# An attention and MLP kernel: softmax normalisation by 32x32 VectorE transposes, four heads of scores per round, and zero matmuls before the input arrives

## The chip, the cores and the metric

The kernel runs on one core of one Trainium2 chip. The metric is the device time of one execution in microseconds (us), as a median over runs. Five engines work side by side: TensorE (PE in the profile; PEld is its weight load), VectorE (DVE), ScalarE (ACT), GpSimd (POOL) and SyncE (SP), which here issues most of the DMAs. TensorE's clock is throttled: the trace has records of a granted clock that is either full or half (in the kernel before, matmuls of 512 columns stand 216 ns apart at full clock and 427 at half).

The kernel before takes 235.04 us (median of three runs, 234.85 to 235.3).

## The reference, cut to what matters

```python
x = A_x                                          # 1 x 2048 x 448, bf16
h  = x + _A_ref(_layernorm(x), A_wqkv, A_wo)     # 16 heads of 28; each query sees 8 keys, every second one back
h2 = h + _B_ref(_layernorm(h), w1, w2, w3, w4)   # token mixing, then an MLP of width 1792
# inside _A_ref
logits = jnp.where(mask, jnp.einsum("bhsd,bhswd->bhsw", q, kg) * scale, -1e9)
attn = _softmax(logits, axis=-1)
o = jnp.einsum("bhsw,bhswd->bhsd", attn, vg)
return o.transpose(...).reshape(B, S, D) @ wo
```

The kernel works on four tiles of 512 tokens, numbered 0 to 3. For each tile: layer norm (A1), transposition of the normalised tile into `hT`, V and QK projections, attention in four groups of four heads (att, av), output projection (WO), a second layer norm (B1), and so on to the MLP (W3, B3). Tile 0 is transposed by TensorE, the others by a DMA transpose. Even and odd tokens lie in different tiles, so that the dilated window becomes a band.

## The kernel before

The 3,650 or so instructions are not written in their order. The program lists operations with estimated durations, and a list scheduler, run when the kernel is built, fixes the order of every engine. Its estimates: a matmul always costs its time at full clock, and a DMA lands after bytes over a fixed bandwidth plus 2 us.

```python
def mm(out_ap, lhsT, rhs, start, stop, n, mode="full"):
    return S.add("pe", "matmul", n / 2.4 + 3 if mode == "full" else 26.0, ...)

    # in _Sched.schedule(self, dma_bw=180.0, slack=100.0): of the ready operations take the one that can start
    # first, ties by rank in _ORDER, a list of some 170 stage names
            if op.is_dma:
                free[e] = st + op.dur
                ts = max(st + op.dur, dma_free[e])
                dma_free[e] = ts + op.lat / dma_bw
                op.t1 = dma_free[e] + 2000.0
            else:
                op.t1 = st + op.dur
                free[e] = op.t1
            order[e].append(op)          # from here on the order is fixed
```

The statistics of a layer norm go from VectorE to GpSimd (a power and three small operations), and each of the four normalisations of a tile to VectorE or ScalarE, whichever the plan has free:

```python
def phase_A1(t):
    for i in range(4 * t, 4 * t + 4):
        ln_stats(0, xin[:, i, :], i)                 # VectorE
        if t == 0:
            inv_std(0, 0, i, 1)                      # GpSimd: four serial chains for tile 0
    if t > 0:
        inv_std(0, 0, 4 * t, 4)
    for il in range(4):
        normalize_t(0, 0, 4 * t + il, ls, il, xin[:, 4 * t + il, :])   # VectorE or ScalarE
    ...
    if t == 0: transposes(ls, hT[:, par, :, :])      # TensorE
    else:      transpose_dma(ls, hT[:, par, :, :])   # DMA
```

Attention, for each group c of four heads. The values have a 29th column that is constant, so row 28 of each 32-row block of the output is the softmax sum:

```python
for jp in range(2):                                  # two heads per round, two PSUM banks
    T = tile(2)
    for q0, nq, k0 in BLK:
        for j in (2 * jp, 2 * jp + 1):
            mm(T(... a=j % 2 ...), qk[32 * j:32 * j + 28, par, c, 1, k0:k0 + KB],
               qk[32 * j:32 * j + 28, par, c, 0, 8 + q0:8 + q0 + nq], True, True, nq, "rows")
    act(pj, T(...), ACT.Exp, 1024, scale=SCALE)
    dve("tensor_tensor", 1024, 2.0, out=pj, in0=pj, in1=m_, op=ALU.mult)        # mask
... # 20 matmuls of attention times V into O; after every second group:
if c % 2 == 1:
    copy(osb[:, par, c - 1:c + 1, :], O(lambda p: p[:, :, :]), 1024)
... # once per tile, after its four groups:
dma("zg%d" % par, zp[:, par, :], zrows, 32768)                      # gather the sums
dve("reciprocal", 400, out=rzp[:, par, :], in_=zp[:, par, :])
dve("tensor_scalar", 64, out=rzp[:, par, :], in0=rzp[:, par, :], scalar1=UP, ...)
dma("zs%d" % par, zd.rearrange("j (r n) -> (j r) n", n=64), rzp[:, par, :], 32768)   # to DRAM
for j in range(4):                                                  # and back, to 32 rows each
    dma("zb%d" % j, rzb[32 * j:32 * j + 32, :, :]..., bass.AP(rz_d, ..., [[0, 32], [1, 2048]]), 32 * 8192)
for c in range(4):
    dve("tensor_tensor", 512, out=oT[:, par, c, :], in0=osb[:, par, c, :], in1=rzb[:, c, :], op=ALU.mult)
```

## Time and profile before

| What | Value | Read from |
|---|---|---|
| time, median | 235.04 us | runs |
| span of the profiled run | 232.0 us | page |
| TensorE busy | 201.1 us, 87% | page, part 1 |
| VectorE, ScalarE, GpSimd busy | 121.6, 117.2, 66.4 us | page, part 1 |
| first real matmul | 13.83 us | timeline |
| 848 full-array matmuls, 189 or 216 ns apart | 171.5 us | trace |
| half clock between the first real matmul and the tail (no record yet counts as half) | 14.5 us | clock records of the trace |
| TensorE's waits from 14 us on | 14.9 us | timeline, sum of the brackets |

TensorE is the engine to look at: it is busy nearly throughout and its clock is sometimes halved. From the page of the kernel before, the span, the busy line and two rows of the table of 40 slices (5.8 us each; the digit is the busy share in tenths, and for PEclk the granted clock in tenths):

```profile
span 232.0 us, 3657 instructions
PE 201.1 (87%) x1505; PEld 102.6 (44%) x1505; DVE 121.6 (52%) x244; ACT 117.2 (50%) x131; POOL 66.4 (29%) x123
PE   0289999999999749499778999999999999999992
PEclk9999999999999967889999999999999999999998
```

The PE row shows an empty start, a thin stretch in slices 14 to 22 (75 to 128 us) and a dense second half. PEclk shows a 9 also where there is no record yet: the first one, of a full clock, stands at 18.13 us, and matmuls before it ran 427 ns apart, at half speed. The timeline of TensorE in the kernel before (start, duration, what, count; in brackets the idle time before it and what ended that):

```profile
6.77 0.46 PE L1197 MATMUL ps<-ident,lntm 128*112 128x128 bf16 x2 [6.77 <-ACT lntm L1197]
...
11.39 1.32 PE L1197 MATMUL ps<-ident,lntm 128*112 128x128 bf16 x10 [1.18 <-DVE lntm L1197]
13.83 6.38 PE L1197 MATMUL ps<-hT,arena 112*128 112x512 bf16 x19 [1.12 <-ACT hT L1197]
```

The transposes of tile 0 come first, then 19 matmuls in 6.38 us, the first of them at half speed. The softmax round trip is seen in the DMA queue's timeline of the kernel before:

```profile
81.85 0.55 SPq L1197 DMA_DIRECT2D zp<-arena  x1
85.27 0.34 SPq L1197 DMA_DIRECT2D rz_scratch<-rzp  x1
86.73 1.70 SPq L1197 DMA_DIRECT2D rzb<-rz_scratch  x4
88.47 4.68 SPq L1197 DMA_TRANSPOSE actT<-lntm  x1
```

This is the third of four tiles: the sums are gathered at 81.85 us, written at 85.27, fetched back from 86.73, and the transposition that follows in the queue comes behind them. Two groups of VectorE in the kernel before, which the change removes (count | busy us, mean ns | idle before):

```profile
L1197 DVE TENSOR_TENSOR oT<-arena,rzb 128x512 bf16<-128x512 f32 x16 | 11.0, 737 | 1.0 <-DMA rzb<-rz_scratch 1.0
L1197 DVE RECIPROCAL rzp<-zp 128x64 f32<-128x64 f32 x4 | 2.2, 547 | 0.3 <-DMA zp<-arena 0.3
```

### The profile page before, as it was taken

The page shows a single profiled execution, that of the slowest core. Times are in us where ns is not written, and L with a number is a line of the kernel's source. Part 1 is how long each engine was busy: PE and PEld are TensorE (multiplying, and loading weights), DVE is VectorE, ACT ScalarE, POOL GpSimd, SP SyncE. Part 2 cuts the span into 40 slices and gives each one's busy share as a digit, 9 for nine tenths or more (in the row PEclk, how much of TensorE's full clock was granted, in tenths as well). Part 3 has the DMA queues.
Part 4 walks back from the last instruction along what each step waited for, and adds up shares of the span by engine and source line. Part 5 has one row for each costly group of instructions (what it writes and reads, how often), then busy time and mean ns, then how long its engine had stood idle before and what let it go on. Part 6 is the DMA issues. An engine that isn't in the chain of part 4 may idle for free.

```text
span 232.0 us, 3657 instructions
## 1 busy us (share of the span) xinstructions
PE 201.1 (87%) x1505; PEld 102.6 (44%) x1505; DVE 121.6 (52%) x244; ACT 117.2 (50%) x131; POOL 66.4 (29%) x123
## 2 busy tenths in 40 slices
PE   0289999999999749499778999999999999999992
PEld 0135564445456424254333455554444455444550
DVE  6494684458859888956889604992100122001221
ACT  2616885578877795495651663214755500353000
POOL 8856374001100610433183500489700000000000
PEclk9999999999999967889999999999999999999998
DMA  5925615976604309447504040041400501001111
GB/s 159 298 66 147 154 28 113 277 241 123 158 6 113 79 11 193 87 83 184 100 8 86 0 90 0 3 90 59 90 3 0 110 20 41 21 0 41 41 45 47
DMA packets 31671, 19.82 MB, mean 85 GB/s; under 512 B 24800, under 2 KB 30256, under 8 KB 31136
## 3 DMA queue, kind: packets, MB, share of 16 engines
q1 hardware_dynamic: 30608, 15.10, 29.0%
q0 software_dynamic: 1040, 4.42, 6.8%
q8 instruction: 14, 0.23, 0.4%
q14 instruction: 9, 0.07, 0.1%
HBM read 11.65 MB, written 1.97 MB: 59 GB/s over the span
## 4 chain that ended last, share of the span: by engine, by line
PE 64%; DVE 14%; ACT 7%; DMA 6%; POOL 5%; issue 2%
PE ps L1197 64%; DVE st L1197 5%; DMA actT<-lntm 4%; ACT pt L1197 3%; POOL rstd L1197 3%; DMA hT<-lntm 3%; DVE xin L1197 3%; POOL nmr L1197 2%; DVE mv L1197 1%; ACT arena L1197 1%; DVE xb L1197 1%; DVE pt L1197 1%; POOL vtmp L1197 1%; ACT qk L1197 1%; DVE lntm L1197 1%
## 5 line engine op out<-in xcount | busy, mean ns | idle before, releaser
L1197 PE MATMUL ps<-actT,w_s 112*128 112x512 bf16 (+1 forms) x288 | 67.5, 386 | 2.8 <-DMA actT<-lntm 2.8
L1197 ACT ACTIVATE arena<-ps 128x1024 bf16<-128x1024 f32 (+1 forms) x34 | 34.8, 1023 | 43.5 <-PE ps L1197 43.3
L1197 DVE TENSOR_TENSOR xb<-ps,xb 128x448 bf16<-128x448 f32 (+1 forms) x24 | 18.3, 771 | 65.5 <-PE ps L1197 65.5
L1197 PEld LDWEIGHTS ps<-actT,w_s 112*128 112x128 bf16 (+1 forms) x288 | 30.4, 107 | 35.5 <-DMA actT<-lntm 4.3
L1197 PE MATMUL ps<-w_s,arena 128*128 128x448 bf16 x224 | 45.0, 353 | 0.0
L1197 PE MATMUL ps<-hT,arena 112*128 112x512 bf16 x128 | 32.0, 400 | 1.5 <-ACT hT L1197 1.1
L1197 ACT ACTIVATE pt<-ps 110x1024 bf16<-110x1024 f32 x32 | 30.5, 1023 | 4.5 <-PE ps L1197 4.4
L1197 PEld LDWEIGHTS ps<-w_s,arena 128*128 128x128 bf16 x224 | 21.9, 98 | 21.2
L1197 DVE TENSOR_TENSOR pt<-pt,msk 110x1024 bf16<-110x1024 bf16 x32 | 21.0, 683 | 12.6 <-ACT pt L1197 12.6
L1197 POOL TENSOR_SCALAR vtmp<-mv 128x4 f32<-128x4 f32 (+1 forms) x19 | 5.2, 276 | 67.9 <-DVE mv L1197 67.0
L1197 DVE BATCH_NORM_STATS2 st<-xin 128x6 f32<-128x448 bf16 x32 | 19.3, 604 | 0.7 <-issue 0.5
L1197 PEld LDWEIGHTS ps<-hT,arena 112*128 112x128 bf16 x128 | 12.1, 102 | 16.9 <-issue 2.8
L1197 POOL TENSOR_TENSOR rstd<-vtmp,mhalf 128x4 f32<-128x4 f32 (+1 forms) x19 | 19.0, 999 | 1.6
L1197 PE MATMUL ps<-wo_s,oT 128*128 128x448 bf16 x64 | 15.2, 393 | 2.9 <-DVE oT L1197 1.7
L1197 POOL TENSOR_TENSOR xb<-xb,xin 128x448 bf16<-128x448 bf16 x16 | 16.7, 1073 | 2.4 <-DVE lntm L1197 1.5
L1197 ACT ACTIVATE lntm<-xin,nmr,rstd 128x448 bf16<-128x448 bf16 x16 | 11.5, 755 | 10.3 <-POOL nmr L1197 10.3
L1197 PE MATMUL ps<-qk 28*110 28x103 bf16 (+1 forms) x320 | 12.1, 220 | 4.8 <-ACT arena L1197 2.6
L1197 ACT ACTIVATE qk<-ps 128x1024 bf16<-128x1024 f32 x10 | 10.2, 1024 | 10.7 <-PE ps L1197 10.7
L1197 PE MATMUL ps<-arena,hT 112*110 112x448 bf16 x64 | 14.9, 358 | 0.4 <-DMA hT<-lntm 0.4
L1197 PE MATMUL ps<-w_s,gT 112*128 112x448 bf16 x64 | 12.8, 353 | 1.4 <-ACT gT L1197 1.4
L1197 PEld LDWEIGHTS ps<-qk 28*110 28x110 bf16 x320 | 9.2, 127 | 10.0 <-ACT arena L1197 3.3
L1197 ACT ACTIVATE gT<-ps 112x1024 bf16<-112x1024 f32 x8 | 8.2, 1024 | 9.0 <-PE ps L1197 9.0
(58 smaller groups left out, 162.7 us busy)
## 6 DMA issues: line engine op xcount, KB each, us to landing
rzb<-rz_scratch SPq DMA_DIRECT2D x16, 256.0 KB, 4.5
w_s<-in_B_w_dram POOLq DMA_DIRECT2D x2, 1568.0 KB, 11.5
out_dram<-xb SPq DMA_DIRECT2D x16, 112.0 KB, 1.7
xin<-in_A_x_dram SPq DMA_DIRECT2D x3, 448.0 KB, 7.9
arena<-in_A_wqkv_dram SPq DMA_DIRECT2D x3, 392.0 KB, 5.3
w_s<-in_B_w_dram POOLq DMA_DIRECT2D x2, 392.0 KB, 4.6
xin<-in_A_x_dram SPq DMA_DIRECT2D x4, 112.0 KB, 2.2
wo_s<-in_A_wo_dram POOLq DMA_DIRECT2D x4, 98.0 KB, 2.5
```

Of the source, the lines that this page charges most:

```text
L1197: inst = getattr(eng, op.meth)(**op.kw)
```

## The change

The intent: keep the softmax sums out of DRAM. A 32x32 transpose on VectorE turns each block of 29 rows by 32 queries so that the sum stands beside its query, where a reciprocal and a broadcast product normalise it; a second transpose turns the block back. Besides: the scores of four heads go in one round on four PSUM banks, tile 0's statistics are taken in pairs, and 14 zero matmuls are to have the clock up when the input arrives. The list of priorities is a new one, so nearly every engine's order changes. The diff, cut to its core:

```diff
-W3_0.04 W3_0.10 W3_0.02 W3_2 ...
+W3_2.04 W3_2.00 W3_2.12 W3_2.08 ...                                  [all 13 lines of _ORDER]
+    WARM = 14
+    zz = sb("zz", [128, 512], BF16)
+    dve("memset", 256, ap=zz[:], constant=0.0)
-            if t == 0:
-                inv_std(0, 0, i, 1)
+            if t == 0 and i % 2 == 1:
+                inv_std(0, 0, i - 1, 2)
...                                                                   [scores]
+            Ts = [tile(2), tile(2)]
+            for q0, nq, k0 in BLK:
+                for j in range(4):
+                    mm(Ts[j // 2](lambda p, a=j % 2, q=q0, n=nq: p[0:KB, a, q:q + n]), ...
             for jp in range(2):
-                T = tile(2)
-                for q0, nq, k0 in BLK:
-                    for j in (2 * jp, 2 * jp + 1):
-                        mm(T(lambda p, a=j % 2, q=q0, n=nq: p[0:KB, a, q:q + n]), ...
-                act(pj, T(lambda p: p[0:KB, :, :]), ACT.Exp, 1024, scale=SCALE)
+                act(pj, Ts[jp](lambda p: p[0:KB, :, :]), ACT.Exp, 1024, scale=SCALE)
...                                                                   [normalisation, two groups at a time]
-                copy(osb[:, par, c - 1:c + 1, :], O(lambda p: p[:, :, :]), 1024)
-        [the gather, the reciprocal, the write, four reads back and four products of the kernel before]
+                dve("transpose", 1024, psum=True, out=of[:, os_, :, :], in_=O(lambda p: p[:, :, :]))
+                o4 = of[:, os_, :, :].rearrange("p u (b d) -> p (u b) d", d=32)
+                dve("reciprocal", 160, out=rz[:, os_, :], in_=o4[:, :, 28])
+                dve("scalar_tensor_tensor", 1024, out=ob[:, os_, :, :]...,
+                    in0=rz[:, os_, :].unsqueeze(2).broadcast_to([128, 32, 32]), scalar=UP, in1=o4, op0=ALU.mult, op1=ALU.mult)
+                dve("transpose", 1024, out=oT[:, par, c - 1:c + 1, :], in_=ob[:, os_, :, :])
...                                                                   [zero matmuls]
+    S.tag = "warm"
+    T = tile()
+    for _ in range(WARM):
+        mm(T(lambda p: p[:, 0, :]), zz[:, 0:128], zz[:], True, True, 800)
     phase_A1(0)
```

A few estimated durations were also corrected (a normalisation on ScalarE from 560 to 755 ns, for example).

More of the change, by code (lines that the diff above doesn't have):

```diff
@@ L20, in __init__ @@
     def __init__(self, idx, eng, meth, kw, dur):
-        self.idx = idx; self.eng = eng; self.meth = meth; self.kw = kw; self.dur = dur
+        self.idx = idx; self.eng = eng; self.meth = meth; self.kw = kw; self.dur = float(int(dur))
         self.deps = set(); self.users = 0; self.sem = None; self.val = 0
@@ L103, in add @@
         if chan is not None:
-            op.is_dma = True; op.chan = chan; op.lat = float(lat)
+            op.is_dma = True; op.chan = chan; op.lat = float(int(lat))
             self.chan_count[chan] = self.chan_count.get(chan, 0) + 1
@@ L256, in schedule @@
                 op.meth, op.kw, op.dur = op.opts[e]
+                op.dur = float(int(op.dur))
             if e == "act" and op.table is not None:
@@ L338 @@
 _ORDER = """
-W3_0.04 W3_0.10 W3_0.02 W3_2 W3_2.10 W3_2.00 W3_2.04 W3_2.08 W3_3.12 W3_3.02 W3_3.08 W3_3.06 B2_0.0 B2_0.2 W3_3
-W3_3.00 W3_3.10 av_2.1 W3_0.00 W3_0 W3_0.06 W3_0.12 W3_0.08 W3_2.12 W3_2.06 W3_2.02 W3_1.02 W3_1.08 W3_1.06 W3_1.04
-W3_1.12 W3_1.00 W3_1.10 QK_3.2 W3_3.04 av_0.1 av_0.0 B2_2.0 att_1.1 rz_2 rz_1 B1_3 WO_2.0 B2_2.2 QK_3 B3_1.3 B2_3.0
-B3_2.1 B2_3.2 B1_3.0 W3_1 att_1.2 B3_2.0 B3_1.1 av_1.0 B3_1.0 B3_1.2 att_2.3 att_3.1 att_3.3 att_3.2 att_3.0 V_1.1
-V_1.3 V_1.0 av_1.1 A1_0 att_2.1 QK_3.1 V_2.1 QK_3.0 B1_1 B3_2.2 WO_0.0 A1_1 QK_3.3 rz_3 B2_1.0 QK_0.1 B3_2.3 att_2.2
-B1_1.0 B1_2.0 B1_2 B1_2.2 att_0.2 B2_1.2 att_2.0 WO_2.2 B1_3.2 QK_2.0 V_3.0 QK_2.2 att_0.3 QK_2.1 att_0.1 B3_0.3
-B1_0.0 WO_3.2 QK_2 B1_0.2 B1_0 WO_1.2 WO_3.0 WO_1.0 QK_0.3 att_0.0 V_3.1 av_3.0 WO_0.2 QK_0.2 B1_1.2 QK_1.1 att_1.3
-QK_1.0 QK_1.3 A1_2 rz_0 B3_3.1 B3_3.3 B3_3.2 B3_3.0 B3_0.1 B3_0.0 att_1.0 V_0.3 av_2.0 V_0.0 QK_1.2 V_0.1 V_3.3
-QK_2.3 av_3.1 QK_0.0 B3_0.2 V_2.0 A1_3 V_2.3
+W3_2.04 W3_2.00 W3_2.12 W3_2.08 W3_2.10 W3_2.02 W3_2.06 W3_2 av_1.0 V_1.3 B3_2.2 av_0.0 att_0.1 att_0.2 att_0.3
+att_0.0 B3_2.3 av_1.1 B3_2.0 B3_2.1 V_0.1 V_0.3 B3_3.0 B3_3.2 B3_3.1 B3_3.3 WO_1.2 WO_1.0 QK_1.3 av_0.1 WO_0.2
+WO_0.0 V_1.0 WO_2.0 WO_2.2 WO_3.0 WO_3.2 att_3.3 QK_0.2 QK_1.0 B3_1.2 att_2.3 QK_0.1 B1_0.2 B1_3.0 B1_1.0 QK_2.1
+att_1.1 att_1.2 att_1.3 att_1.0 W3_1.00 W3_1.06 W3_1.08 W3_3.00 W3_3.02 W3_3.04 W3_3.08 W3_3.10 W3_3 W3_1.12 W3_3.06
+QK_2.2 W3_3.12 B3_1.3 B3_1.0 B3_1.1 att_2.1 B1_3.2 B1_3 V_1.1 att_2.2 QK_1.2 att_2.0 QK_0.3 W3_1.02 W3_1.04 W3_1.10
+W3_0.04 B1_1 B1_1.2 V_3.1 QK_2 QK_1.1 B1_0.0 W3_0.10 QK_3 W3_1 QK_3.3 QK_3.1 QK_3.0 A1_1 W3_0.00 W3_0.08 B2_0.0 A1_0
+QK_2.3 mask QK_3.2 av_2.1 B2_2.2 B3_0.3 A1_2 B2_2.0 W3_0.02 B2_0.2 V_0.0 av_2.0 av_3.1 B1_2.2 QK_2.0 att_3.1 W3_0.06
+B2_3.0 V_3.0 B3_0.0 B1_2 att_3.2 V_3.3 W3_0.12 QK_0.0 av_3.0 V_2.1 V_2.0 B3_0.1 B1_0 att_3.0 B2_1.2 B2_1.0 W3_0
+B2_3.2 B3_0.2 A1_3 load V_2.3 B1_2.0 init
 """
@@ L363, in _fast_path @@
     S = _Sched()
+    S.tag = "init"
     def sb(name, shape, dt):
@@ L368, in _fast_path @@
     R_WQ = 4 * (1024 + 3 * D)
-    R_OS = 2 * 4 * 512 * 2
-    AR = sb("arena", [128, R_WQ + R_OS], BF16)
+    R_H3 = NF * 512
+    AR = sb("arena", [128, R_WQ + R_H3], BF16)
     def arv(off, parts, n):
@@ L376, in _fast_path @@
     wqkv_s = arv(4096, KC, 4 * 3 * D).rearrange("p (c n) -> p c n", c=4)
-    osb = arv(R_WQ, 128, R_OS).bitcast(F32).rearrange("p (s c n) -> p s c n", s=2, c=4)
+    of = arv(R_WQ, 128, 4096).bitcast(F32).rearrange("p (s u n) -> p s u n", s=2, u=2)
+    ob = arv(R_WQ + 4096, 128, 2048).rearrange("p (s u n) -> p s u n", s=2, u=2)
     h3T = [arv(o, 128, NF * 512).rearrange("p (f n) -> p f n", f=NF) for o in (0, R_WQ)]
@@ L385, in _fast_path @@
     oT = sb("oT", [128, 2, 4, 512], BF16)
-    rzb = sb("rzb", [128, 4, 512], F32)
     gT = sb("gT", [KC, 4, 2, HALF + 2], BF16)
@@ L391, in _fast_path @@
     actT = sb("actT", [128, 2, 4, 512], BF16)
-    zp = sb("zp", [128, 2, 64], F32)
-    rzp = sb("rzp", [128, 2, 64], F32)
+    rz = sb("rz", [128, 2, 32], F32)
+    zz = sb("zz", [128, 512], BF16)
     msk = sb("msk", [128, 2, 512], BF16)
@@ L411, in _fast_path @@
     ps = es.enter_context(nc.psum_tensor("ps", [128, 8, 512], F32))
-    rz_d = nc.dram_tensor("rz_scratch", (NST * 4, 2048), F32, kind="Internal")
     def mm(out_ap, lhsT, rhs, start, stop, n, mode="full"):
@@ L481, in masks @@
     def masks():
+        S.tag = "mask"
         mv4 = msk[:, :, 0:412].rearrange("p v (b q) -> p v b q", q=103)
@@ L508, in _fast_path @@
     uctr = [0]
+    octr = [0]
     def ln_stats(kind, src, i):
-        dve("bn_stats", D, out=st6[:, kind, i, :], in_=src)
+        dve("bn_stats", D + 20, out=st6[:, kind, i, :], in_=src)
         dve("bn_aggr", 64, out=mv[:, kind, i, :], in_=st6[:, kind, i, :])
@@ L529, in normalize @@
             "dve": ("tensor_scalar", dict(out=out_ap, in0=in_ap, scalar1=m_, scalar2=r_, op0=ALU.subtract, op1=ALU.mult), 390),
-            "act": ("activation", dict(out=out_ap, in_=in_ap, func=ACT.Identity, scale=r_, bias=n_), 560)})
+            "act": ("activation", dict(out=out_ap, in_=in_ap, func=ACT.Identity, scale=r_, bias=n_), 755)})
     def normalize_t(slot, kind, i, ls, il, src):
@@ L615, in phase_att @@
             uctr[0] += 1
-            for jp in range(2):
-                T = tile(2)
-                for q0, nq, k0 in BLK:
-                    for j in (2 * jp, 2 * jp + 1):
-                        mm(T(lambda p, a=j % 2, q=q0, n=nq: p[0:KB, a, q:q + n]),
-                           qk[32 * j:32 * j + 28, par, c, 1, k0:k0 + KB],
-                           qk[32 * j:32 * j + 28, par, c, 0, 8 + q0:8 + q0 + nq], True, True, nq, "rows")
+            Ts = [tile(2), tile(2)]
+            for q0, nq, k0 in BLK:
+                for j in range(4):
+                    mm(Ts[j // 2](lambda p, a=j % 2, q=q0, n=nq: p[0:KB, a, q:q + n]),
+                       qk[32 * j:32 * j + 28, par, c, 1, k0:k0 + KB],
+                       qk[32 * j:32 * j + 28, par, c, 0, 8 + q0:8 + q0 + nq], True, True, nq, "rows")
+            for jp in range(2):
                 pj = pt[0:KB, sl, 2 * jp:2 * jp + 2, :]
-                act(pj, T(lambda p: p[0:KB, :, :]), ACT.Exp, 1024, scale=SCALE)
+                act(pj, Ts[jp](lambda p: p[0:KB, :, :]), ACT.Exp, 1024, scale=SCALE)
                 m_ = msk[0:KB, 0 if h == 0 else 1, :].unsqueeze(1).broadcast_to([KB, 2, 512])
-                dve("tensor_tensor", 1024, 2.0, out=pj, in0=pj, in1=m_, op=ALU.mult)
+                dve("tensor_tensor", 1024, 1.9, out=pj, in0=pj, in1=m_, op=ALU.mult)
             S.tag = "av_%d.%d" % (t, c // 2)
@@ L634, in phase_att @@
             if c % 2 == 1:
-                copy(osb[:, par, c - 1:c + 1, :], O(lambda p: p[:, :, :]), 1024)
-        S.tag = "rz_%d" % t
-        zrows = osb[28:128:32, par, :, :].rearrange("p c n -> p (c n)").rearrange("p (r n) -> p r n", n=64)
-        dma("zg%d" % par, zp[:, par, :], zrows, 32768)
-        dve("reciprocal", 400, out=rzp[:, par, :], in_=zp[:, par, :])
-        dve("tensor_scalar", 64, out=rzp[:, par, :], in0=rzp[:, par, :], scalar1=UP, scalar2=None, op0=ALU.mult)
-        zd = rz_d.ap()[4 * t:4 * t + 4, :]
-        dma("zs%d" % par, zd.rearrange("j (r n) -> (j r) n", n=64), rzp[:, par, :], 32768)
-        for j in range(4):
-            dma("zb%d" % j, rzb[32 * j:32 * j + 32, :, :].rearrange("p c n -> p (c n)"),
-                bass.AP(rz_d, (4 * t + j) * 2048, [[0, 32], [1, 2048]]), 32 * 8192)
-        for c in range(4):
-            dve("tensor_tensor", 512, out=oT[:, par, c, :], in0=osb[:, par, c, :], in1=rzb[:, c, :], op=ALU.mult)
+                os_ = octr[0] % 2
+                octr[0] += 1
+                dve("transpose", 1024, psum=True, out=of[:, os_, :, :], in_=O(lambda p: p[:, :, :]))
+                o4 = of[:, os_, :, :].rearrange("p u (b d) -> p (u b) d", d=32)
+                dve("reciprocal", 160, out=rz[:, os_, :], in_=o4[:, :, 28])
+                dve("scalar_tensor_tensor", 1024, out=ob[:, os_, :, :].rearrange("p u (b d) -> p (u b) d", d=32),
+                    in0=rz[:, os_, :].unsqueeze(2).broadcast_to([128, 32, 32]), scalar=UP, in1=o4, op0=ALU.mult, op1=ALU.mult)
+                dve("transpose", 1024, out=oT[:, par, c - 1:c + 1, :], in_=ob[:, os_, :, :])
     def phase_WO(t):
@@ L753, in behind @@
         S.after = S.ops[-1]
+        S.tag = "load"
         load()
         S.after = None
+    S.tag = "warm"
+    T = tile()
+    for _ in range(WARM):
+        mm(T(lambda p: p[:, 0, :]), zz[:, 0:128], zz[:], True, True, 800)
     phase_A1(0)
@@ L797, in _fast_path @@
     S.rank = {tag: i for i, tag in enumerate(_ORDER.split())}
-    S.rank["flag"] = -1
+    S.rank["flag"] = S.rank["warm"] = -1
     return S, flag_op
```

## The prediction

> **What bounds the kernel now.** TensorE. The page shows PE busy 87% of a 232.0 us span; the chain of waits gives it 64%. In the trace the 848 full-array matmuls stand 189 ns (448 columns, 432 of them) or 216 ns (512 columns, 416) apart when nothing holds them: 171.5 us. Scores and attention-times-V take about 20 us. The other 40 us are loss: the first real matmul starts at 13.8 us (timeline); 4.6 us of tail; PE waits in between of about 15 us, 8 of them between 79 and 97 us; and the clock. The first full-clock record stands at 18.1 us, so matmuls from 13.8 to 18.1 us ran 427 ns apart: 2.1 us lost. Two later falls to half (83 to 90, 97 to 100 us) cost about 3 us.
>
> **What the change does.**
>
> 1. Softmax sums no longer go through DRAM. From the gather of a tile's sums to its first oT product 14 to 20 us pass, four times (DMA queue's timeline: 47.8 to 63.2, 67.2 to 82.7, 81.9 to 95.9, 96.4 to 116.3). Removed: 16 broadcasts of 256 KB; beside one set a DMA transpose took 8.3 us to land instead of 4.3, on the chain. Added per pair of head groups, on VectorE: a transpose from PSUM (estimate 1.2 us, as a 1024-element f32 copy takes 1.22), a reciprocal of 32 (0.3, from 0.55 for 64), a product of 1024 f32 (1.15, from 0.69 for 512), a bf16 transpose[...]: 3.9 us x 8 = 31. Gone from VectorE: 11 us of oT products, 3 of reciprocals and scalings, 2.4 of copies; from ScalarE 6.1. Net VectorE +14 us, less copies that move to ScalarE. VectorE was idle about 25 us between 34 and 122 us: it fits, tightly. Latency from last head to oT: 4 to 6 us. WO and B1 come free earlier; I expect 3 to 7 us back from PE's waits and cold clock around 80 to 125 us.
>
> 2. Twenty score matmuls take 0.5 us joined, 0.78 in two separate groups[...]: gain 2 to 3 us, partly lost to holding four PSUM banks.
>
> 3. Zero matmuls (14 x 427 ns = 6 us, in idle time): the clock should be up when work starts[...]. Gain 2 us.
>
> 4. First tile's statistics in pairs: GpSimd's four serial chains of 1.4 us become two of about 1.6: start 2 to 3 us earlier.
>
> 5. New priorities; the dense last 98 us are untouched.
>
> Sum, less 1 to 2 for busier VectorE: about 13 us.
>
> **Predicted: 221.5 us, 80% range 213 to 230. Faster by over 2%: 0.92; within 2%: 0.06; slower: 0.02.**
>
> **Checks.** Full clock before the first QK or V matmul, at 10.5 to 11.5 us; VectorE busy 130 to 138 us, ScalarE 110 to 116; DMA bytes down by 4.2 MB or more; no DMA transpose over 5 us; PE waits after the start at most 11 us; VectorE transposes 1.1 to 1.3 us each.
>
> **What would make it wrong.** A transpose costing twice the estimate; VectorE pacing attention, so that masks queue behind transposes; PSUM starved by four-bank scores; the clock dropping between zeros and real work; a schedule, fixed by estimated durations, that fits the chip worse.

Where the recorded text is cut, it gave times or reasons that no trace of the kernel before shows. Its sum, about 13 us, stands as recorded, and two terms inside it are cut: the time of the bf16 transpose, an estimate of the author's that is counted in the 3.9 us of step 1 (the three terms left come to 2.65 us), and the time of twenty score matmuls with four heads per round, an estimate too, on which the 2 to 3 us of step 2 partly rested. The reason why zeros would bring the clock up is cut as well; what the trace of the kernel before shows is a first full-clock record at 18.13 us, 4.3 us after the first real matmul, and the 2 us of step 3 are the 2.1 us lost at half clock there.

## The result, and the profile after

The kernel after takes 234.94 us (median of 4 runs, 234.73 to 235.2); the kernel before took 235.17 in the same rounds (4 runs, 234.85 to 235.63). The ratio is 0.9989, with a 95% interval of 0.9968 to 1.001: the same time. Ratios here and below are the mean time of one kernel's fast runs over that of the other's of the same rounds, so not quite the ratio of the medians quoted. Executions over 1.5% slower than the fastest of the same kernel are left out of the means. From the page of the kernel after:

```profile
span 233.0 us, 3646 instructions
PE 207.8 (89%) x1519; PEld 105.8 (45%) x1519; DVE 132.4 (57%) x244; ACT 120.1 (52%) x134; POOL 61.1 (26%) x115
PE   7499589898988984999588999999999999999991
PEclk9769958999999995699889999999999999999998
```

Slices 14 to 22 of the PE row are denser than before (984999588 against 749499778), which is what removing the round trip was for. But there is a new dip to 5 in slice 5, and PEclk dips three times instead of twice after the start: 5 and 8 in slices 6 and 7 are new. VectorE's new groups in the kernel after:

```profile
L1201 DVE SCALAR_TENSOR_TENSOR arena<-rz,arena 128x1024 bf16<-128x1024 f32 x8 | 10.7, 1334 | 0.2
L1201 DVE STREAM_TRANSPOSE oT<-arena 128x1024 bf16<-128x1024 bf16 x8 | 10.0, 1245 | 0.3
L1201 DVE STREAM_TRANSPOSE arena<-ps 128x1024 f32<-128x1024 f32 x8 | 9.9, 1235 | 4.1 <-PE ps L1201 4.1
L1201 DVE RECIPROCAL rz<-arena 128x32 f32<-128x32 f32 x8 | 2.8, 346 | 0.2
```

The four steps take 1.235 + 0.346 + 1.334 + 1.245 = 4.16 us, eight times 33 us, where 31 were predicted. A transpose of 1024 elements per lane took about the same from f32 in PSUM (1.235 us) as from bf16 in SBUF (1.245), which is about 1.2 ns per element of a lane, as a plain copy of 1024 f32 elements does (1.22). VectorE's total rose by 10.8 us. So the added work was sized about right; whether it paces the kernel is tested below. The start of TensorE in the kernel after:

```profile
1.33 5.30 PE L1201 MATMUL ps<-zz 128*128 128x512 bf16 x14 [1.33 <-DVE qk L1201]
7.42 0.43 PE L1201 MATMUL ps<-ident,lntm 128*112 128x128 bf16 x4 [0.79 <-ACT lntm L1201]
9.30 1.53 PE L1201 MATMUL ps<-ident,lntm 128*112 128x128 bf16 x12 [1.45 <-ACT lntm L1201]
11.94 3.61 PE L1201 MATMUL ps<-arena,hT 112*110 112x448 bf16 x9 [1.11 <-ACT hT L1201]
```

Real work starts 1.9 us earlier than before (11.94 for 13.83). The zeros did release the clock: the records say full from 5.63 us, 4.3 us after the first zero, to 9.04 us (with the zeros cut to one column, in z_off below, the first full clock came at 17.1 us). But it was half again from 9.04 to 15.87 us, just when the real work began: 9 matmuls of 448 columns in 3.61 us is twice the 189 ns apart of full speed. Between the last zero (6.63) and the first real matmul TensorE had only 16 short transposes, and the clock fell 2.4 us after that zero. (The short records of this trace last 3.41, 6.83 or 10.24 us.) With 11 zero matmuls between and behind the same transposes, in z_thru below, it stayed full to 26.44 us. The transposes here were short and apart, so whether a transpose counts for the clock as a matmul does, no run shows.

What follows is the stall of slice 5. TensorE's timeline in the kernel after, then ScalarE's and GpSimd's:

```profile
25.70 0.46 PE L1201 MATMUL ps<-qk 28*110 28x103 bf16 x10
27.08 0.46 PE L1201 MATMUL ps<-qk 28*110 28x103 bf16 x20 [0.93 <-DVE qk L1201]
30.11 1.34 PE L1201 MATMUL ps<-arena,hT 112*110 112x448 bf16 x3 [2.57 <-DMA hT<-lntm]
```

```profile
17.13 0.92 ACT L1201 ACTIVATE vt<-ps 110x896 bf16<-110x896 f32 x1 [1.00 <-PE ps L1201]
18.86 1.02 ACT L1201 ACTIVATE qk<-ps 128x1024 bf16<-128x1024 f32 x1 [0.81 <-PE ps L1201]
20.59 1.02 ACT L1201 ACTIVATE qk<-ps 128x1024 bf16<-128x1024 f32 x1 [0.70 <-PE ps L1201]
21.51 1.40 ACT L1201 ACTIVATE lntm<-xin,nmr,rstd 128x448 bf16<-128x448 bf16 x2
```

```profile
15.66 0.20 POOL L1201 TENSOR_TENSOR nmr<-nmr,rstd 128x4 f32<-128x4 f32 x1
```

Read them together. GpSimd has the statistics of tile 1 ready at 15.86 us. ScalarE's two normalisations of that tile need nothing else, but they stand in its order behind three copies (17.13, 18.86, 20.59) that each wait for TensorE, which is at half speed. They run at 21.51 us, the DMA transpose is issued at 22.93 and lands at 30.0, and TensorE waits 2.57 us for it (after 0.93 us for VectorE). Within that wait the clock falls again, and it is half from 29.52 to 36.35 us, with real work going on. In the kernel before, tile 1's transpose was issued at 21.95 and landed at 28.1, and TensorE waited 0.36 us.

The plan explains the order. (Its times are those that the scheduler sets down when the kernel is built; they stand in no trace.) In it those copies came at 15.24, 16.97 and 18.70 us, and tile 1's statistics only at 19.15 us, so the normalisations went behind them at no cost. On the chip the copies came 1.9 us later than planned and the statistics 3.3 us earlier.

The next table is worked out from the traces. It gives every matmul its time at full clock (189 ns for 448 columns, 216 for 512, 20 for one of scores, 18 for one of attention times V, about 56 for one of tile 0's 16 transposes; in all 184.6 us) and sums up what had been started by a time t. It shows who is ahead, whatever the order of the work.

| started by t (us) | before | after | early | both2 | b_sound |
|---|---|---|---|---|---|
| 20 | 5.0 | 7.2 | 7.4 | 9.3 | 6.1 |
| 30 | 14.1 | 12.8 | 15.6 | 17.4 | 15.6 |
| 36 | 19.6 | 15.8 | 21.5 | 23.1 | 20.5 |
| 40 | 23.3 | 19.6 | 24.6 | 26.3 | 23.7 |
| 75 | 53.3 | 49.7 | 55.0 | 56.6 | 53.8 |
| 85 | 57.0 | 58.2 | 59.8 | 59.9 | 57.2 |
| 100 | 63.6 | 64.4 | 69.8 | 71.7 | 64.0 |
| 160 | 117.4 | 117.0 | 122.3 | 124.2 | 117.2 |

(The last three columns are experiments told below.) The kernel after leads by 2.2 us at 20 us and is 3.8 behind at 36: a swing of 6 us within 16. It catches up 5 us between 36 and 85 us, nearly all of it after 75, and ends level. A second account, of the same traces, in us (the wait just before the first real matmul is part of the first row alone):

| | before | after | both2 | b_sound |
|---|---|---|---|---|
| first real matmul | 13.83 | 11.94 | 11.29 | 13.63 |
| TensorE's waits, 14 to 76 us | 1.8 | 6.1 | 3.7 | 3.1 |
| TensorE's waits, 76 to 122 us | 12.0 | 7.2 | 9.5 | 12.4 |
| waits after 122 us | 1.2 | 1.8 | 0.0 | 1.2 |
| half clock, first real matmul to tail | 14.5 | 24.4 | 13.7 | 13.7 |

The kernel after starts 1.9 us earlier and saves 4.7 us of waits in the attention stretch. It loses 4.3 us by waits before that, 0.5 later, and has 9.9 us more of half clock, which is up to 4.9 us of work (less where TensorE also waits). The sum is 1.9 + 4.7 − 4.3 − 0.5 − 4.9 = −3.1 at worst, and the profiled span is 1.0 longer, so the account is good to about 2 us. The gain was real and was given back, and the question for the chip is which loss is a property of the change and which an accident of its order.

### The profile page after: what moved, and what is told of

The parts are those of the page before. It is cut to its first block, busy times and chain, and to the rows that moved or that the text cites. A ratio compares the mean times of both kernels' runs of the same rounds, so it can differ in the third digit from the quotient of the medians.

```text
span 233.0 us, 3646 instructions
## 1 busy us (share of the span) xinstructions
PE 207.8 (89%) x1519; PEld 105.8 (45%) x1519; DVE 132.4 (57%) x244; ACT 120.1 (52%) x134; POOL 61.1 (26%) x115
## 2 busy tenths in 40 slices
DMA packets 29798, 15.36 MB, mean 66 GB/s; under 512 B 23440, under 2 KB 28896, under 8 KB 29776
## 4 chain that ended last, share of the span: by engine, by line
PE 69%; DVE 13%; ACT 5%; POOL 5%; DMA 3%; issue 2%; POOLq 0%
PE ps L1201 69%; DVE arena L1201 3%; DMA hT<-lntm 3%; ACT pt L1201 3%; DVE st L1201 3%; POOL rstd L1201 2%; DVE pt L1201 2%; DVE xin L1201 2%; ACT qk L1201 1%; POOL nmr L1201 1%; DVE xb L1201 1%; DVE oT L1201 1%; POOL msk L1201 1%; DVE mv L1201 1%; POOL vtmp L1201 1%
## 5 line engine op out<-in xcount | busy, mean ns | idle before, releaser
L1201 PE MATMUL ps<-actT,w_s 112*128 112x512 bf16 (+1 forms) x288 | 68.6, 391 | 0.2 <-ACT pt L1201 0.2
L1201 ACT ACTIVATE arena<-ps 128x1024 bf16<-128x1024 f32 x28 | 28.6, 1022 | 44.7 <-PE ps L1201 44.6
L1201 POOL TENSOR_SCALAR vtmp<-mv 128x4 f32<-128x4 f32 (+1 forms) x17 | 3.6, 213 | 69.2 <-DVE mv L1201 68.5
L1201 PE MATMUL ps<-arena,hT 112*110 112x448 bf16 x64 | 17.7, 423 | 4.4 <-DMA hT<-lntm 2.6
L1201 DVE TENSOR_TENSOR pt<-pt,msk 110x1024 bf16<-110x1024 bf16 x32 | 20.4, 676 | 0.3 <-ACT pt L1201 0.2
L1201 ACT ACTIVATE qk<-ps 128x1024 bf16<-128x1024 f32 x13 | 13.3, 1023 | 11.7 <-PE ps L1201 11.7
L1201 POOL TENSOR_TENSOR rstd<-vtmp,mhalf 128x4 f32<-128x4 f32 (+1 forms) x17 | 17.4, 1021 | 1.4
L1201 ACT ACTIVATE lntm<-xin,nmr,rstd 128x448 bf16<-128x448 bf16 x17 | 12.4, 757 | 5.8 <-POOL nmr L1201 5.6
L1201 PE MATMUL ps<-wo_s,oT 128*128 128x448 bf16 x64 | 13.1, 355 | 1.9 <-DVE oT L1201 1.8
L1201 PEld LDWEIGHTS ps<-arena,hT 112*110 112x110 bf16 x64 | 9.3, 154 | 10.7 <-ACT pt L1201 3.4
L1201 PE MATMUL ps<-w_s,gT 112*128 112x448 bf16 x64 | 13.1, 353 | 0.0
```

The source lines that it names most:

```text
L1201: inst = getattr(eng, op.meth)(**op.kw)
```

## The experiments

My theory: the gain is lost at the start, in a chain: the clock falls in the gap behind the zeros, half speed makes the copies late, ScalarE's fixed order makes tile 1 late, and the stall drops the clock again. A first rival: VectorE's 11 us more, which is VectorE pacing attention. A second: four-bank scores that starve PSUM. A third: late landing of DMA transposes beside the weight loads.

Every experiment edits the finished order or adds operations that count nothing in the plan, so all else keeps its place. Fourteen kernels ran, in four batches: z_off, z_thru, early, both; both2, heavy, light, two; b_both, exp31, both2_two, exp31_two; b_sound, a_loads. Each has four runs, the profiled one among them, and each batch seven of the kernel before on the same chip (one chip for the first two batches, another for the last two; medians 235.31, 234.52, 235.64 and 234.66 us; one run of the first batch took 1132.79 us and is in no ratio). Ratios are to the kernel before of the same batch, and runs are fast ones unless the text says otherwise. All but light give the right result.

### z_off: the zero matmuls cut to one column

```diff
-        mm(T(lambda p: p[:, 0, :]), zz[:, 0:128], zz[:], True, True, 800)
+        mm(T(lambda p: p[:, 0, 0:1]), zz[:, 0:128], zz[:, 0:1], True, True, 800)
```

> The changed kernel with its 14 zero matmuls cut to one column each; every engine's order is kept. Both theories: no change against the changed kernel (234.9 us, within 0.7 us), because its clock fell back to half at 9.0 us, before the first real matmul at 11.9 us. If the zeros had helped, the time rises by up to 2 us.

Measured 235.23 us, ratio to before 1.0019 (0.9949 to 1.0089), against 0.9989 for the kernel after. The first full clock came at 17.1 us instead of 5.63 and 15.87. So the 14 zeros are worth nothing that the runs can tell.

### z_thru: the clock held up to the real work

Zeros are added behind tile 0's fourth transpose and behind the last; they cost nothing in the plan.

```diff
-    WARM = 14
+    WARM, MID, END = 18, 6, 5          # before the transposes, behind the 4th, behind the 16th
```

> The changed kernel with 18 zero matmuls, then 6 more between the transposes of the first tile and 5 behind them, so that TensorE has no long pause before real work; orders kept. The clock should be full from about 5.6 us on, and the first 18 real matmuls 189 instead of 373 ns apart, 2 us earlier. Start theory (a late tile 1 starves TensorE at 26 to 30 us, and the clock falls again): tile 1's normalisations come 2 us earlier, so its transpose also lands 2 us earlier; gain about 2 us, the stall stays: 233. VectorE theory (VectorE paces the attention stage): under 0.5 us gained.

Measured 231.93 us, ratio 0.9873 (0.978 to 0.997). TensorE's timeline of z_thru:

```profile
10.03 1.24 PE L1210 MATMUL ps<-zz 128*128 128x512 bf16 x5
11.31 3.23 PE L1210 MATMUL ps<-arena,hT 112*110 112x448 bf16 x16
...
26.83 3.21 PE L1210 MATMUL ps<-arena,hT 112*110 112x448 bf16 x8 [1.84 <-DMA hT<-lntm]
```

Now 16 matmuls take 3.23 us, not 9 in 3.61: full speed from the first one. The clock stays full from 5.96 to 26.44 us. Then tile 1 is late still, and it falls until 33.27. Holding the clock is worth something, and the stall is a loss of its own.

### early: tile 1's normalisations moved ahead on ScalarE

```diff
+def _early(S, order):
+    # both ScalarE normalisations of tile 1 go in front of the copy of tile 0's second pair of V blocks
+    q = order["act"]
+    mv = [op for op in q if op.tag == "A1_1"]
+    for op in mv:
+        q.remove(op)
+    i = next(k for k, op in enumerate(q) if op.tag == "V_0.3")
+    q[i:i] = mv
+    _regorder(S, order)                # only re-sorts the list that semaphores are numbered from
     order = S.schedule()
+    _early(S, order)
```

> The changed kernel with the two ScalarE normalisations of tile 1 moved in front of copies that wait for tile 0's matmuls; nothing else moves. Tile 1's transpose should issue at 17.5 instead of 22.9 us and land by 24. Start theory: the wait at 27.5 to 30.1 us goes, the clock stays full at 29.5 to 36.4 us, together 5 to 6 us by 40 us, of which at least 3 remain at the end: 229 to 232 us. VectorE theory: the gain at 40 us is eaten by later waits for VectorE, 234 us or more.

Measured 230.47 us, ratio 0.9815 (0.9748 to 0.9883): 4.4 us less than before (0.0185 of 235.3) for two instructions moved, with the zeros left as they were. ScalarE's and then TensorE's timeline of early:

```profile
16.20 1.41 ACT L1228 ACTIVATE lntm<-xin,nmr,rstd 128x448 bf16<-128x448 bf16 x2 [0.71 <-POOL nmr L1228]
17.52 0.90 ACT L1228 ACTIVATE vt<-ps 110x896 bf16<-110x896 f32 x1
```

```profile
26.90 0.46 PE L1228 MATMUL ps<-qk 28*110 28x103 bf16 x20 [0.93 <-DVE qk L1228]
27.29 1.72 PE L1228 MATMUL ps<-arena,hT 112*110 112x448 bf16 x8
```

The transpose is issued at 17.64 us, lands at 22.0, and tile 1's matmuls follow without a wait; no half clock from 14.57 to 82.84. In the table of work, early is 5.0 us ahead of the kernel after at 40 us and 5.2 at 160: what is gained here is kept to the end. (The same 14 zeros held the clock to 11.16 us in this trace and to 9.04 in that of the kernel after, and no run shows why; the lead at 20 us is 0.2 us all the same.)

### both: z_thru and early together

The two edits at once.

> Both edits: zeros through the start and tile 1 normalised early. Start theory: gains add, 7 us ahead at 40 us, 227 to 230 us at the end. VectorE theory: 233.5 us or more, with VectorE busy over 90% from 56 to 128 us and TensorE waiting for it.

Measured 232.13 us, ratio 0.987 (0.979 to 0.995), which is no better than early. A miss of mine in the edit: with the clock up, TensorE is ready sooner, and the copy that now stands behind the two normalisations waits with them for GpSimd's statistics. TensorE's timeline of both:

```profile
18.47 1.89 PE L1237 MATMUL ps<-hT,arena 112*128 112x512 bf16 x4 [2.23 <-ACT vt L1237]
```

It had a wait of 2.23 us, and the clock fell from 18.38 to 21.8 us. The place that was right in early, where the first real matmuls ran at half clock, was wrong here, where they ran at full clock.

### both2: the same, with the normalisations one copy later

```diff
-    i = next(k for k, op in enumerate(q) if op.tag == "V_0.3")
+    i = next(k for k, op in enumerate(q) if op.tag == "QK_0.2")
```

> Zeros through the start, and tile 1 normalised early, but one place later on ScalarE than in the run called both: behind the second V copy, in front of the Q and K copies. In both, that copy waited for GpSimd and TensorE starved at 16 to 18 us. Start theory: no wait at 16 to 18 us, the clock stays full from 6 to 80 us, 2 us ahead of early at 40 us, end 228 to 229.5 us. VectorE theory: no better than early (230.5).

Measured 227.78 us, ratio 0.9713 (0.966 to 0.9766): 6.7 us or 2.9% faster than before. Full clock from 5.79 to 80.88 us without a break. Against early (0.9815) the held clock adds about 2.4 us (0.0102 of 235), close to the 2 us that the prediction gave to it; but the two intervals just overlap, and the normalisations also stand one copy later than in early. By the ratios, against the kernel after (0.9989), mending the gap behind the zeros alone gives 2.7 us (z_thru), ScalarE's order alone 4.1 (early), both 6.5 (both2). So both losses at the start are shown, each by an edit that touches nothing else.

### heavy and light: is VectorE the limit?

Both stand on early. heavy does the normalising product twice (8 more of it, about 10 us); light masks only 64 of 512 columns, which takes about 15 us from VectorE and is wrong (relative error 1.018).

```diff
 heavy:
+                dve("scalar_tensor_tensor", -110, ...the same operation again...)
 light:
-                dve("tensor_tensor", 1024, 1.9, out=pj, in0=pj, in1=m_, op=ALU.mult)
+                dve("tensor_tensor", 1024, 1.9, out=pj[:, :, 0:64], in0=pj[:, :, 0:64], in1=m_[:, :, 0:64], op=ALU.mult)
```

> The early kernel with each of the eight normalising products done twice: 10 us more VectorE work, all of it in the attention stage, 1.2 us more latency in each chain. VectorE theory (VectorE paces from 56 to 124 us): 5 us or more slower than early, 235 or more. Start theory alone: it costs at most 2 us, 231 to 232.5.

> The early kernel with the masks applied to 64 of 512 columns only; the result is wrong on purpose. VectorE loses about 15 us of work between 25 and 113 us, orders kept. VectorE theory: 4 us or more faster than early, 226 or less. Start theory alone: at most 1.5 us faster, 229 to 230.5.

heavy took 236.22 us, 1.0068 (1.0015 to 1.012), which is 5.7 us more than early's 230.47 (5.9 by the ratios); light 228.66, 0.9703 (0.9627 to 0.978; one of its four runs slow and left out), 2.6 us less than early by the ratios. So about 0.6 us per us added, and under 0.2 us per us removed. heavy came out as the VectorE theory had it, light between the two theories, with an interval that overlaps early's. heavy's product also stands in the chain from the last head to oT and makes it 1.3 us longer, so it does not part VectorE's load from that delay: TensorE's waits for oT rose from 1.5 us in early to 4.7. What the pair shows is that VectorE has little to spare after the 11 us that the change gave it. As the rival for the lost gain it falls short: 15 us less of it buy 2.6 us at most, two instructions moved on ScalarE bought 4.1.

### two: scores of two heads per round again

On early, TensorE's order within each group is put back to two heads and then two.

```diff
+        ops = sorted((q[i] for i in k), key=lambda op: op.idx)          # k: the 20 places of a group's scores
+        first = ops[0].group
+        ops = [op for op in ops if op.group is first] + [op for op in ops if op.group is not first]
```

> The early kernel with the scores of two heads per round again, in the same places of TensorE's order: only the order inside each set of twenty score matmuls changes. The prediction gave four heads 2 to 3 us: then this run is 232 to 233.5. If the gain is off the path or eaten by PSUM, it is within 0.7 us of early, 230 to 231.

Measured 229.29 us, ratio 0.9757 (0.9708 to 0.9806), against early's 0.9815. The intervals overlap, so no more can be said than that four heads gain nothing. The traces show why so little was to be had. From the start of one score matmul to the start of the next, less waits, the 320 score matmuls take 10.8 us in the kernel before, 10.1 in early and 10.5 in two: a set of twenty in one run takes 0.51 us in early and 0.58 in two (0.54 in the kernel before), where the prediction set 0.5 against 0.78. The 0.78 is twice the time of a set of ten alone (0.39), and between such sets TensorE did other work. TensorE's waits for exponentials, in early and then in two:

```profile
PE ps L1228 <- ACT pt L1228: 7.2, 6, 3.2
PE ps L1242 <- ACT pt L1242: 7.0, 5, 3.4
```

They stay. The edit leaves the sets of twenty at their places and the banks as the plan gave them, so it shows that the order of four heads is not what these waits come from; what it costs to hold four banks at a time, it does not test.

### b_both: the same start in the kernel before

To see what the change is worth apart from its start, the kernel before gets the same sound start: zeros put into TensorE's finished order (18 first, then 5 behind the 2nd, 4th, 6th and 16th transpose) and tile 1's normalisations in front of the QK_0.3 copy.

```diff
+    for n, at in ((first, tr[0]), (mid, tr[2]), (mid, tr[4]), (mid, tr[6]), (mid, q[q.index(tr[-1]) + 1])):
+        for _ in range(n):
+            q.insert(q.index(at), new("pe", "matmul", {z}, out=ps[:, bank, :], lhsT=zz[:, 0:128], rhs=zz[:], ...))
```

> The kernel before, orders kept, with the repairs of the start alone: zero matmuls up to its first real matmul (one extra VectorE memset), and tile 1's ScalarE normalisations one copy earlier. It has none of the change's softmax, four-head scores or paired statistics. If those are worth nothing even with a sound start: 228 to 229, as both2. If the prediction's term for softmax (3 to 7 us) and for paired statistics (2 to 3) holds: 232 to 233.5, 2 us better than before for the clock alone.

Measured 237.6 us, ratio 1.0086 (1.0022 to 1.0151): 0.9% slower. A miss, and it teaches something. TensorE's timeline of b_both:

```profile
29.68 1.77 PE L1251 MATMUL ps<-arena,hT 112*110 112x448 bf16 x7 [2.88 <-DMA hT<-lntm]
```

The transpose was issued at 19.07 us, 2.9 us earlier than before, and still landed only at 29.6, after 10.5 us instead of the 4.4 of early. It now ran beside the loads of `wo`, `w1` and `w2`, issued from 17.5 to 21.6 us. So this did not test what it was for; it raised the third rival again.

### exp31, both2_two and exp31_two

What is left of the attention stretch in the changed kernel: TensorE's longest wait, 3.16 us before 92.73 in the kernel after and before 84.95 in both2. All eight PSUM banks hold scores of tile 3 at that point (29 sets of ten have been multiplied and 25 exponentials have ended, and each of the four sets between holds two banks), and the exponential that would free some stands on ScalarE behind layer norm work. In the kernel after (GpSimd's timeline, then VectorE's, then ScalarE's):

```profile
87.97 0.20 POOL L1201 TENSOR_TENSOR nmr<-nmr,rstd 128x4 f32<-128x4 f32 x1
...
89.86 1.12 POOL L1201 TENSOR_TENSOR nmr<-nmr,rstd 128x4 f32<-128x4 f32 x1
```

```profile
89.69 1.23 DVE L1201 SCALAR_TENSOR_TENSOR arena<-rz,arena 128x1024 bf16<-128x1024 f32 x1
```

```profile
91.01 0.76 ACT L1201 ACTIVATE xb<-xin,nmr,rstd 128x448 bf16<-128x448 bf16 x1 [1.40 <-POOL nmr L1201]
91.68 4.66 ACT L1201 ACTIVATE pt<-ps 110x1024 bf16<-110x1024 f32 x5
```

The same small GpSimd operation takes 0.20 us at one time and 1.12 at another, when it starts inside the new normalising product and ends 0.06 us after it (90.98 and 90.92). At every other place in this trace the GpSimd operation took 0.19 to 0.20 us, beside VectorE's transposes and statistics too. The kernel before has the same in small: 0.49 us where the operation starts inside a mask product of VectorE (79.38 to 80.06 us) and ends 0.06 us after it, and 0.36 where it starts inside a VectorE copy (8.47 to 8.86 us) and ends 0.05 us after that. Why the operation takes longer there, no run shows. ScalarE waits 1.40 us for the GpSimd operation, and the exponentials come behind. A round of four heads writes to four banks in this program, and all eight are held here.

exp31 moves the two exponentials of att_3.1 ahead of the layer norm work that begins with B1_1 on ScalarE, on top of both2; both2_two and exp31_two add the order of two heads.

```diff
+    mv = [op for op in q if op.tag == "att_3.1"]          # _exp31: the same move as _early
+    i = next(k for k, op in enumerate(q) if op.tag == "B1_1")
```

> both2 with two exponentials of tile 3 (group 1) moved on ScalarE in front of layer norm work, nothing else. At 81.8 to 85.0 us TensorE has no PSUM left: the scores of tile 3 hold all eight banks, and the exponential that frees two of them sits behind an operation that waits for GpSimd. If that wait is what costs there: 1.5 to 3 us faster than both2, 225 to 226.5. If VectorE paces that stretch: no change.

> both2 with two heads per round of scores in the same places. Four heads worth 2 to 3 us: 230 to 231. Four heads worth nothing, as in the pair early and two: 227 to 228.5.

> exp31 with two heads per round: the version that should be best if four heads are worth nothing, 224.5 to 227; if the sets of four heads matter once the wait at 82 us is gone, slower than exp31 by 1 us or more.

exp31 took 227.9 us, 0.9692 (0.9636 to 0.9749): no clear gain over both2's 0.9713, and a miss (225 to 226.5 expected). Its trace shows the wait gone (waits for exponentials 3.8 us for 7.2), but a new one of 1.8 us for a normalisation of ScalarE behind it, and the half clock as before (13.7 us). both2_two took 230.07 in the median of four, of which two were slow, the profiled one among them; its fast runs give 0.9677 (0.9591 to 0.9764). exp31_two took 226.41 us (225.72 to 227.4), 0.9637 (0.9573 to 0.9701): the fastest version of all, 3.6% faster than the kernel before. In all three pairs (early and two, both2 and both2_two, exp31 and exp31_two; only the last within one batch) two heads are ahead of four by 0.4 to 0.6%, each inside its intervals. So the four-head round is worth nothing, and may cost a little.

### b_sound and a_loads: the loads kept away from the transpose

By then 12 runs were used and the cause was not settled: what of the loss was ScalarE's order, and what the late landing? In both kernels the loads of `wo`, `w1` and `w2` are moved behind the landing of tile 1's transpose on GpSimd's queue. b_sound is b_both with that and 14 first zeros; a_loads is the kernel after with that alone.

```diff
+    mv = [op for op in q if op.is_dma and op.chan in ("wo0", "wo1", "wo2", "wo3", "w1", "w2")]      # q: GpSimd's order
+    i = 1 + max(k for k, op in enumerate(q) if op.tag == "A1_1" and op.meth == "tensor_copy")
+    q[i:i] = mv
```

> b_both with the loads of three weights moved on GpSimd's queue behind the landing of tile 1's DMA transpose, and 14 instead of 18 first zeros. In b_both that transpose took 10.5 us to land among the loads (4.4 alone) and TensorE starved at 26.8 to 29.7 us. Loads theory: it lands in 5 us, no wait there, the clock stays full to 80 us, and the kernel before with a sound start is 232 to 233.5, 2 us better than before and 4 to 6 us behind both2: the part of the forecast that softmax, paired statistics and their order are worth. If softmax is worth nothing: 228 to 229.

> The changed kernel with the same loads moved behind the landing of tile 1's transpose, nothing else: ScalarE's order is as in the change, so the transpose still issues at 22.9 us. Loads theory: it lands in 4.4 instead of 7.0 us, at 27.3, the wait before 30.1 us shrinks from 2.6 to 0.5 us and the clock does not fall at 29.5: 230.5 to 232.5. If the late ScalarE work alone is to blame: 234 to 235.

a_loads took 233.68 us (231.84 to 235.93, one of four slow), ratio 0.9917 (0.9846 to 0.9987). The transpose was issued at 23.03 us and landed at 29.2; with no load beside it that is still 6.1 us, not 4.4. TensorE's timeline of a_loads:

```profile
29.30 2.04 PE L1239 MATMUL ps<-arena,hT 112*110 112x448 bf16 x6 [1.66 <-DMA hT<-lntm]
```

The stall shrank from 2.57 to 1.66 us and the clock fell all the same, at 29.7 us. So the loads cost some 0.9 us of this landing (7.0 to 6.1; one trace each) and at most about 1.7 us of time (0.9917 for 0.9989, intervals that overlap), and ScalarE's order, which early repaired by itself for 4.1 us, is the larger cause. Transposes beside loads land late elsewhere too: those of tiles 2 and 3 land in 4.2 to 4.5 us with no load beside them, and tile 3's, which in every version of the change runs beside more than 2 MB of weights, in 12.0 to 13.1 us. TensorE does not wait for that one. In the trace of a_loads the transpose's packets of one microsecond (25 to 26 us) took some 66 ns each where others took 21, and one 16 KB packet of instruction fetch fell in that time; b_sound shows the same at 22 us, where its transpose took 5.9 us. That is a coincidence in a few traces and not a shown cause.

b_sound took 233.79 us, ratio 0.9962 (0.9908 to 1.0015). Its clock is full from 5.79 to 80.88 us, as both2's, and half for 13.7 us after that, as both2's. So here the two kernels can be compared with equally sound starts and equal times of half clock: 0.9713 against 0.9962, about 2.5% or 5.9 us, for what the change does apart from its zeros (b_sound also has its loads moved, both2 does not). In the second account above, 2.3 us is the earlier first matmul (11.29 for 13.63; the statistics in pairs and the new order), and 3.6 are fewer waits: about 3 between 76 and 122 us and 1.2 later, less 0.6 lost before. (The two profiled spans differ by 7.1 us, so 1.2 us of that pair are not accounted for.) TensorE's waits in b_sound, and then in both2 (total us, times, longest):

```profile
PE ps L1263 <- ACT arena L1263: 5.2, 4, 2.2
PE ps L1263 <- DMA actT<-lntm: 3.1, 3, 2.0
```

```profile
PE ps L1237 <- ACT pt L1237: 7.2, 6, 3.2
PE ps L1237 <- DVE arena L1237: 2.0, 4, 0.8
```

The waits for ScalarE's copies of attention's output and for the transposes that queued behind the sums are gone. In their place TensorE waits for exponentials (7.2 us, for 2.3 in b_sound), which is PSUM held by scores. Two waits make up most of it. The first is the one before 84.95 us told above. The second comes from the new priorities: they put tile 3's last two exponentials behind activations of the later stage (gT), so ScalarE loads its function tables four times, 1.28 us each, where the kernel before loads them twice. ScalarE and then TensorE in both2:

```profile
104.38 1.28 ACT L1237 ACT_TABLE_LOAD   x1
105.68 1.94 ACT L1237 ACTIVATE pt<-ps 110x1024 bf16<-110x1024 f32 x2
```

```profile
107.67 0.46 PE L1237 MATMUL ps<-pt,vt 110*32 110x103 bf16 x22 [2.75 <-ACT pt L1237]
```

The after kernel and exp31 have the same wait (2.74 us each); no run moves these exponentials. The kernel before profited from its sound start by only 0.9 us, which is not clear of noise: b_sound leads it by 1.5 us of work at 30 us, but by 0.4 at 40, 75 and 100 us. So most of the lead is gone long before the round trip of the sums; no run shows why.

## Why the prediction was wrong

It said 221.5 us, 213 to 230, with 0.92 for faster by over 2%. It came out at 234.94, the same as before. What failed is how steps 3 and 4 were added to the sum, and step 2; what the runs showed in their place follows, step by step.

- **Step 1, the softmax, held.** The costs on VectorE were right: transposes 1.235 and 1.245 us (1.1 to 1.3 expected), the sum 4.16 us for 3.9, VectorE busy 132.4 us (130 to 138 expected), DMA bytes down from 19.82 to 15.36 MB (4.2 or more expected). "It fits, tightly" was right too (heavy and light). The 3 to 7 us from waits are there: 4.7 us fewer between 76 and 122 us in the kernel after, about 3 in both2 against b_sound. The new order of priorities is in that difference as well; no run parts them. ScalarE went up to 120.1 us, where 110 to 116 was expected: its two more table loads take 2.6 us and three more copies of Q and K 3.1, and neither was in the sum.
- **Step 2, four heads, failed.** The term that was wrong is "0.5 us joined, 0.78 in two separate groups": in the order of two heads twenty score matmuls in one run take 0.54 to 0.58 us, so joining them saves 0.4 to 0.8 us in the whole kernel (early against two, exp31 against exp31_two), not 2 to 3. Three pairs of runs give nothing or a small loss. The starvation of PSUM that the prediction named is there (the wait of 3.2 us in early and both2), but it stays with the order of two heads (3.4 us in two) and goes when two exponentials move (exp31); whether holding four banks at a time adds to it is not tested.
- **Step 3, the zeros, failed.** That activity releases the clock was right here (full from 5.63 us in the kernel after, from 17.1 in z_off). "The clock should be up when work starts" was not: 5.3 us passed between the last zero and the first real matmul, and the clock was half again from 9.04 us. Worth: 0 (z_off). Held through the gap, 2.4 to 2.7 us (both2 over early, z_thru over after), so the size was right and the length was not.
- **Step 4, the earlier start, was right in itself and failed in the sum.** The start was 1.9 us earlier (2 to 3 expected; no run parts the pairs from the new order). But TensorE has a finite stock of tile 0's work, and it ran dry before tile 1 came, since tile 1 came later (30.0 for 28.1 us). From a lead of 2.2 us at 20 us came 3.8 us of arrears at 36. The prediction added the earlier start to the total without asking what feeds TensorE next. This step, with step 3, is the failure: repaired, it gives 1.7% alone (early) and 2.8% with the clock held (both2 over after, 0.9713 over 0.9989).
- **Step 5 and the last sentence.** "A schedule, fixed by estimated durations, that fits the chip worse" and "the clock dropping between zeros and real work" were both listed as dangers and both came, and together got 8% of the weight. The check "no DMA transpose over 5 us" failed as well (7.0 us for tile 1 and 12.0 for tile 3, for which TensorE did not wait; the kernel before had 6.2 and 4.2), and so did "PE waits after the start at most 11 us" (15.1). A list of dangers is no use unless it widens the range.
- **The sum of about 13 us was too large anyway.** With the start mended the change is worth 6.7 us (both2), and 8.5 us with two more edits (exp31_two, 0.0363 of 235). The missing part is step 2 and the half clock of the attention stretch, which stayed at 13.7 us in every sound version.

Still open: why tile 1's transpose needs 6.1 us at 23 us with no load beside it and 4.4 at 17 us; how much of the second fall of the clock the two more table loads cost; whether two heads are really ahead of four; and what would keep the clock up between 80 and 112 us, where every version still drops to half at least twice.

## What to carry to other kernels

Warming the clock paid here only when activity reached without a long gap to the first real matmul (0 us gained with a gap of 5.3 us in the kernel after, 2.7 without it in z_thru); look at the clock records at that moment, not at the zeros. When one stage gets faster, find what the fast engine needs next and whether that also comes earlier: in an order fixed from estimates, ready work can stand behind copies that wait for the very engine you tried to feed. A sum of separately costed gains needs such a check at every seam, and the dangers you list should be in the odds.
